# The third pair's last 32 tokens of keys as four loads of 117, 5, 5 and 1 rows, and VectorE's first block at the end of its program

## The chip, the cores and the metric

The kernel runs on one core of a Trainium2 chip. The core has five engines that run their own programs and meet at semaphores: TensorE (PE, matmuls), VectorE (DVE), ScalarE (ACT), GpSimd (POOL) and SyncE (SP), which here only issues transfers. Sixteen DMA engines move data between the chip's main memory (HBM) and the on-chip memory (SBUF), which has 128 partitions, here also called rows. The metric is the device time of one execution in microseconds, and the median of several runs stands for a kernel.

## The reference

One decode step of a transformer block: a vector `c` modulates it, attention reads a cache of 16,384 tokens in 32 heads, and a gated MLP follows. Everything is bf16, for a single token.

```python
mod = (_silu(c) @ w_mod).reshape(c.shape[0], 6, 1, -1)     # c (1, 640), w_mod (640, 3840)
h = _layernorm(x) * (1 + ca) + sa                           # x (1, 1, 640)
q = (h @ wq) as 32 heads of 128                             # wq (640, 4096)
p = softmax(q . k_cache * 128 ** -0.5)                      # k_cache (1, 32, 16384, 128)
x = x + ga * ((p . v_cache) @ wo)                           # v_cache like k_cache, wo (4096, 640)
h = _layernorm(x) * (1 + cb) + sb
x = x + gb * ((silu(h @ w_gate) * (h @ w_up)) @ w_down)     # (640, 1728) twice, (1728, 640)
```

The two caches are 134 MB each; the weights together some 22 MB.

## The kernel before

The heads are worked through in 16 pairs. For one pair the keys are 128 rows of 256 tokens (64 rows a head), each token 128 values of 2 bytes: a row is 64 KB, contiguous in HBM, and a pair is 8.39 MB. `kring` holds the keys of two pairs (slot `p % 2`), `vbuf` the values of one; the last pair's values go into a slot of `kring`.

For each pair VectorE multiplies the keys by the query, spread over all rows in `qbc` (L544 in the two halves c = 0 and 1 of a pair, L562 for the first and the last pair), and folds the products of a token twice (L549, L554; three times in L568). PE sums what is left of each token into scores (`reduce_mm`, L534; `reduce_end`, L576). `largest` and `weigh` make the softmax weights `PZ`, and `pv` (L508) multiplies them with the values. Pairs 1 to 14 run in a loop on PE; on VectorE and ScalarE pairs 0 to 2 are written out and 3 to 14 are a loop of six turns with two pairs in each. After the last pair the output projection, the second layer norm, gate, up and down follow, and two small transfers write the result.

`_Plan` records every operation with what it depends on, and `emit` writes out one program for each engine. Operations of an engine stay in the order of their recording, so nothing is scheduled. A wait goes ahead of the operation that needs it, unless the same engine has waited for as much before. Each transfer counts on a semaphore of its own channel: `("k", p % 2, c)` is that of piece `c` of the keys of pair `p`, so slots share channels. SP issues transfers in recorded order: w_mod, wq, the keys of pair 0 in two pieces (`KCUT`), the keys of pair 1, the values of pair 0, the keys of pair 2, and so on in turns; all of these transfers start at L90. The keys of pair `p` wait for the reduction of pair `p - 2` (`o_R`), the values of pair `p` for `pv` of pair `p - 1`. The last transfers are wo in two pieces, gate, up and five pieces of w_down.

The programs of ScalarE, VectorE and PE stand in blocks of their own: a branch in the main block (L203) leads to `go_act`, `go_dve` and `go_pe`, which come one behind the other in memory. VectorE's program begins with a memset of one row of `rl` (L352, named `one1`); the next is that of `ones_f` (L353). The lines that the prediction's steps touch are `load_k` (L488), `score` (L539, with the wait for the keys at L546), `run` inside `emit` (L139) and the branches (L198 to L206).

Of the kernel before, what the change touches and what calls it, by code (L numbers as in the profile page):

```python
# [37 lines left out]
class _Plan:  # L38
# [7 lines left out]
    def __init__(self, nc, es):  # L46
        self.nc = nc
        self.es = es
        self.ops = []
        self.loop = {}  # L50
        self.turn = None
        self.chans = {e: _Chan(es.enter_context(nc.semaphore("ch_" + e)), 1) for e in self.ENGS if e != "sp"}
        self.dma_chans = {}

# [22 lines left out]
    def op(self, eng, fn, deps=(), name="", chan=None):  # L77
        o = _Op(eng, fn, list(deps), name, len(self.ops), self.loop.get(eng), chan)
        o.sig = chan is not None
        self.ops.append(o)  # L80
        return o
# [23 lines left out]
    def emit(self):  # L105
        for o in self.ops:
            for d in o.deps:
                d.sig = True
                assert d.seq < o.seq, (o.name, d.name)
        per_eng = {e: [o for o in self.ops if o.eng == e] for e in self.ENGS}  # L110
        for e in self.ENGS:
            by_place = {}
            for o in per_eng[e]:
                if o.loop:
                    key, i, n = o.loop
                    by_place.setdefault((key, i), []).append(o)
            for (key, i), ops in by_place.items():
                first = by_place[(key, 0)]
                assert len(first) == len(ops), (key, i)
                for a, b in zip(first, ops):  # L120
                    a.sig = a.sig or b.sig
            for (key, i), ops in by_place.items():
                for a, b in zip(by_place[(key, 0)], ops):
                    b.sig = a.sig
            for o in per_eng[e]:
                if o.sig:
                    ch = o.chan if o.chan is not None else self.chans[e]
                    o.chan = ch
                    ch.count += ch.inc
                    ch.ops.append(o)  # L130
                    o.val = ch.count

        def issue(eng, o):
            ins = o.fn(eng)
            if o.sig:
                assert ins is not None, o.name
                ins.then_inc(o.chan.sem, o.chan.inc)

        def run(name, eng):  # L139
            known = {}  # L140
            ops = per_eng[name]
            at = 0
            while at < len(ops):
                o = ops[at]
                if o.loop is None:
                    for k, (ch, v) in self.needs(o).items():
                        if known.get(k, 0) < v:
                            eng.wait_ge(ch.sem, v)
                            known[k] = v
                    issue(eng, o)  # L150
                    at += 1
                    continue
                key, i, n = o.loop
                end = at
                while end < len(ops) and ops[end].loop and ops[end].loop[0] == key:
                    end += 1
                body = (end - at) // n
                rows = [ops[at + j * body:at + (j + 1) * body] for j in range(n)]
                assert (end - at) == body * n and all(x.loop[1] == j for j, r in enumerate(rows) for x in r)
                done = {}  # L160
                body_needs = []
                for b in range(body):
                    each = [self.needs(r[b]) for r in rows]
                    assert all(set(x) == set(each[1]) for x in each[1:]), rows[0][b].name
                    for k, (ch, v) in each[0].items():
                        if k not in each[1]:

                            assert ch.ops[v // ch.inc - 1].seq < ops[at].seq, rows[0][b].name
                            if known.get(k, 0) < v:
                                eng.wait_ge(ch.sem, v)  # L170
                                known[k] = v
                    waits = []
                    for k, (ch, v1) in each[1].items():
                        step = each[2][k][1] - v1
                        v0 = v1 - step
                        assert all(x[k][1] == v0 + j * step for j, x in enumerate(each) if j), (rows[0][b].name, [x[k][1] for x in each])
                        assert v0 > 0 and step >= 0
                        assert k not in each[0] or each[0][k][1] <= v0, rows[0][b].name
                        assert v0 % ch.inc == 0 and ch.ops[v0 // ch.inc - 1].seq < rows[0][b].seq, rows[0][b].name
                        if known.get(k, 0) >= each[-1][k][1]:  # L180
                            continue
                        if k in done and done[k][1] == step and done[k][0] >= v0:
                            continue
                        done[k] = (v0, step)
                        waits.append((ch, v0, step))
                    body_needs.append(waits)
                with eng.Fori(0, n) as it:
                    self.turn = it
                    for b in range(body):
                        for ch, v0, step in body_needs[b]:  # L190
                            eng.wait_ge(ch.sem, v0 if step == 0 else it * step + v0)  # L191
                        issue(eng, rows[0][b])
                    self.turn = None
                for k, (v0, step) in done.items():
                    known[k] = max(known.get(k, 0), v0 + (n - 1) * step)
                at = end

        nc = self.nc  # L198
        run("sp", nc.sync)
        run("pool", nc.gpsimd)  # L200
        looped = [(nc.scalar, "act"), (nc.vector, "dve"), (nc.tensor, "pe")]
        for eng, name in looped:
            nc.br("go_" + name, engines=[eng.engine])  # L203
        for eng, name in looped:
            with nc.body("go_" + name, valid_engines=[eng.engine]):
                run(name, eng)  # L206


def build(nc, A_x, A_k, A_v, A_wq, A_wo, B_wg, B_wu, B_wd, c_in, w_mod, out):
# [6 lines left out]
    T2 = 2 * S // 128  # L216
# [16 lines left out]
    with es:  # L233
        plan = _Plan(nc, es)
        op, dma = plan.op, plan.dma
# [5 lines left out]
        kring = sb("kring", [128, 2, T2, 128], BF16)  # L241
# [216 lines left out]
        o_qev = []  # L458
# [22 lines left out]
        d_k, d_v = [None] * NP, [None] * NP  # L481
        o_R, o_pv, o_exp, o_nb, o_mx, o_acc, o_ot = ([None] * NP for _ in range(7))
        KCUT = [0, T2 // 2, T2]
        LCUT = [0, T2 // 2, 7 * T2 // 8, T2]
        VCUT = [0, T2]
        v_at = lambda p: vbuf[:] if p < NP - 1 else kring[:, 0]

        def load_k(p):  # L488
            deps = [o_R[p - 2]] if p >= 2 else ([o_mod[1]] if p == 1 else [])
            cuts = KCUT if p == 0 else [0, T2]  # L490
            d_k[p] = [dma(kring[:, p % 2, a:b], k_src(p)[:, a:b], ("k", p % 2, c), deps=deps, name="dma_k%d_%d" % (p, c))
                      for c, (a, b) in enumerate(zip(cuts, cuts[1:]))]

        def load_v(p):
            deps = [o_R[NP - 2]] if p == NP - 1 else [o_pv[p - 1]] if p >= 1 else [o_q[-1]]
# [43 lines left out]
        def score(p, c, between=None):  # L539

            kv4 = kring[:, p % 2].rearrange("p t (a d) -> p t a d", a=2)[:, :, :, QW * c:QW * c + QW]
            def f_mult(e):
                q4 = qbc[:, bass.ds(plan.at(p), 1), :].rearrange("p o (a d) -> p o a d", a=2)[:, :, :, QW * c:QW * c + QW].broadcast_to([128, T2, 2, QW])
                return e.tensor_tensor(out=kv4, in0=kv4, in1=q4, op=ALU.mult)  # L544
            o_m = op(DVE, f_mult,
                     deps=[d_k[p][-1]] + o_qev[p // 2], name="mult%d_%d" % (p, c))  # L546
            if between:
                between[0]()
            o_f = op(DVE, lambda e: e.tensor_tensor(out=kv4[:, :, 0], in0=kv4[:, :, 0], in1=kv4[:, :, 1], op=ALU.add),  # L549
                     deps=[o_m], name="fold%d_%d" % (p, c))  # L550
            if between:
                between[1]()
            lo = kv4[:, :, 0]
            return op(DVE, lambda e: e.tensor_tensor(out=lo[:, :, 0:QR], in0=lo[:, :, 0:QR], in1=lo[:, :, QR:QW], op=ALU.add),  # L554
                      deps=[o_f], name="fold%d_%db" % (p, c))
# [191 lines left out]
        for i, (b, r0, r1) in enumerate(DOWN):  # L747
# [14 lines left out]
            if i == 0:  # L762
# [7 lines left out]
        d_outs = [dma(o_dst[0:2], o_row[31:33, :], "out0", deps=[o_or], name="dma_out0"),  # L770
                  dma(o_dst[2:4], o_row[95:97, :], "out1", deps=[o_or], name="dma_out1", eng="act")]
        op("sp", lambda e: e.nop(), deps=d_outs, name="final_wait")
        plan.emit()
    return plan

# [45 lines left out]
```

## Time and profile before

| | us |
|---|---|
| median of 3 runs | 679.21 (679.02 to 679.4) |
| the profiled execution | 678.87 |
| its span, first to last instruction | 677.6 |
| PE busy with matmuls | 363.6 (54%) |
| VectorE busy | 514.1 (76%) |
| ScalarE busy | 46.4 (7%) |
| HBM read | 290.47 MB, 429 GB/s over the span |

The profile is of one execution. "Busy" is time in which an engine runs instructions of the program. The rows of groups give a line of the kernel, the engine, the operation, output and inputs, then busy time and mean duration, then the engine's idle time ahead of them and what ended it. A row of windows gives, for one stretch of time, the busy time of PE, PE's weight loads, VectorE, ScalarE and GpSimd, the clock granted to PE, the mean busy share of the 16 DMA engines, and their rate. In a short window that share can pass 1, since a packet's time is counted at its start and consecutive packets overlap a little. DMA queues are listed by number: q1 carries what SP issues, q10 what ScalarE issues, q8 and q14 instructions of the programs; packets, megabytes and their share of 16 engines' time follow.

### The profile page before, as it was taken

The page shows a single profiled execution, that of the slowest core. Times are in us where ns is not written, and L with a number is a line of the kernel's source. Part 1 is how long each engine was busy: PE and PEld are TensorE (multiplying, and loading weights), DVE is VectorE, ACT ScalarE, POOL GpSimd, SP SyncE. Part 2 cuts the span into 40 slices and gives each one's busy share as a digit, 9 for nine tenths or more (in the row PEclk, how much of TensorE's full clock was granted, in tenths as well). Part 3 has the DMA queues.
Part 4 walks back from the last instruction along what each step waited for, and adds up shares of the span by engine and source line. Part 5 has one row for each costly group of instructions (what it writes and reads, how often), then busy time and mean ns, then how long its engine had stood idle before and what let it go on. Part 6 is the DMA issues. An engine that isn't in the chain of part 4 may idle for free.

```text
span 677.6 us, 5406 instructions
## 1 busy us (share of the span) xinstructions
PE 363.6 (54%) x2069; PEld 144.5 (21%) x2069; DVE 514.1 (76%) x190; ACT 46.4 (7%) x146; POOL 0.7 (0%) x6
## 2 busy tenths in 40 slices
PE   2420475755728284654818375562828465481776
PEld 1100122221212122221302122121212222130335
DVE  2189997959596896959597795959699695959912
ACT  1120000100000000000000010000000000000010
POOL 0000000000000000000000000000000000000000
PEclk9675565555757565565756556575656556565765
DMA  9999999999999999999999999999999999999997
GB/s 375 440 459 433 433 437 430 433 430 433 433 434 433 433 433 433 433 433 433 433 433 433 433 433 433 433 433 433 433 433 433 433 433 433 433 433 433 430 400 318
DMA packets 6355, 290.58 MB, mean 429 GB/s; under 512 B 714, under 2 KB 972, under 8 KB 1356
## 3 DMA queue, kind: packets, MB, share of 16 engines
q1 hardware_dynamic: 6340, 290.48, 99.3%
q8 instruction: 5, 0.08, 0.0%
q14 instruction: 2, 0.02, 0.0%
q10 hardware_dynamic: 8, 0.00, 0.0%
HBM read 290.47 MB, written 0.00 MB: 429 GB/s over the span
## 4 chain that ended last, share of the span: by engine, by line
DMA 49%; DVE 30%; issue 13%; PE 8%; SPq 0%; DVEq 0%
DMA kring<-in_A_k_cache_dram 45%; DVE kring L544 10%; PE psb L534 7%; DVE kring L549 6%; DVE kring L562 5%; DVE kring L568 5%; DMA kring<-in_B_w_down_dram 4%; DVE kring L554 3%; SPq L90 0%; DVE pm L581 0%; DVE nb L589 0%; PE psb L576 0%; PE psb L758 0%; DVEq L191 0%; DVEq L544 0%
## 5 line engine op out<-in xcount | busy, mean ns | idle before, releaser
L544 DVE TENSOR_TENSOR kring<-kring,qbc 128x16384 bf16<-128x16384 bf16 x28 | 243.3, 8690 | 96.1 <-DMA kring<-in_A_k_cache_dram 96.1
L534 PE MATMUL psb<-kring,ident 128*128 x448 | 197.5, 607 | 120.3 <-DVE kring L554 120.3
L549 DVE TENSOR_TENSOR kring<-kring 128x8192 bf16<-128x8192 bf16 x28 | 123.8, 4421 | 0.5
L534 PEld LDWEIGHTS psb<-kring,ident 128*128 128x128 bf16 x448 | 54.0, 120 | 248.0 <-issue 247.2
L508 PE MATMUL psb<-vbuf,PZ 128*8 128x512 bf16 x960 | 80.9, 511 | 0.0
L585 PE MATMUL psb<-d,bd_f 128*128 128x64 f32 x32 | 11.0, 446 | 118.5 <-ACT d L583 118.5
L554 DVE TENSOR_TENSOR kring<-kring 128x4096 bf16<-128x4096 bf16 x28 | 64.1, 2288 | 0.5
L562 DVE TENSOR_TENSOR kring<-kring,qbc 128x16384 bf16<-128x16384 bf16 (+2 forms) x5 | 34.9, 6981 | 23.4 <-DMA kring<-in_A_k_cache_dram 23.4
L508 PEld LDWEIGHTS psb<-vbuf,PZ 128*8 128x8 bf16 x960 | 26.6, 108 | 58.9 <-issue 49.0
L576 PE MATMUL psb<-kring,ident 128*128 128x256 bf16 (+3 forms) x64 | 14.5, 392 | 43.2 <-DVE kring L568 43.2
L585 PEld LDWEIGHTS psb<-d,bd_f 128*128 128x128 f32 x32 | 8.0, 312 | 120.7 <-DVE pm L581 111.3
L568 DVE TENSOR_TENSOR kring<-kring 128x2048 bf16<-128x2048 bf16 (+7 forms) x15 | 32.2, 2148 | 0.4
L523 PEld LDWEIGHTS psb<-sel,acc_sb 128*128 128x128 f32 x128 | 28.5, 311 | 7.7 <-issue 4.3
L523 PE MATMUL psb<-sel,acc_sb 128*128 128x2 f32 x128 | 25.6, 322 | 1.1 <-ACT acc_sb L514 1.1
L514 ACT ACTIVATE acc_sb<-psb 128x512 f32<-128x512 f32 x16 | 9.6, 598 | 210.7 <-PE psb L508 210.7
L593 ACT ACTIVATE PZ<-psb,nb 64x256 bf16<-64x256 f32 x32 | 15.0, 469 | 64.8 <-DVE nb L589 64.6
L576 PEld LDWEIGHTS psb<-kring,ident 128*128 128x128 bf16 x64 | 6.4, 121 | 50.5 <-DVE kring L568 44.3
L583 ACT ACTIVATE d<-negid,pm 128x64 f32<-128x64 f32 x16 | 5.6, 348 | 153.2 <-DVE pm L581 153.2
L466 PE MATMUL psb<-vbuf,h_col 128*128 128x512 bf16 x40 | 10.9, 443 | 8.6 <-DMA vbuf<-in_A_wq_dram 8.6
L527 ACT ACTIVATE OT_sb<-psb 128x2 f32 (+1 forms) x16 | 2.8, 172 | 152.2 <-PE psb L523 152.2
L581 DVE TENSOR_REDUCE pm<-psb 128x1 f32<-128x256 f32 x16 | 6.7, 419 | 1.2 <-PE psb L576 1.2
L466 PEld LDWEIGHTS psb<-vbuf,h_col 128*128 128x128 bf16 x40 | 4.1, 112 | 15.3 <-DMA vbuf<-in_A_wq_dram 9.0
(105 smaller groups left out, 79.2 us busy)
## 6 DMA issues: line engine op xcount, KB each, us to landing
kring<-in_A_k_cache_dram SPq DMA_DIRECT2D x2, 4096.0 KB, 40.1
vbuf<-in_A_wq_dram SPq DMA_DIRECT2D x1, 5120.0 KB, 25.8
kring<-in_w_mod_dram SPq DMA_DIRECT2D x1, 4800.0 KB, 14.1
vbuf<-in_A_wo_dram SPq DMA_DIRECT2D x1, 3200.0 KB, 20.6
kring<-in_B_w_gate_dram SPq DMA_DIRECT2D x1, 2160.0 KB, 20.6
kring<-in_B_w_up_dram SPq DMA_DIRECT2D x1, 2160.0 KB, 25.4
vbuf<-in_A_wo_dram SPq DMA_DIRECT2D x1, 1920.0 KB, 24.8
kring<-in_B_w_down_dram SPq DMA_DIRECT2D x3, 640.0 KB, 27.6
```

The costliest lines, as they stand in the source:

```text
L466: last = e.matmul(q_ps[b][:, 0:512], lhsT=h_col[:, k:k + 1].broadcast_to([128, 128]), rhs=wq_v[:, k, g * 512:(g + 1) * 512], start=(k == 0 ...
L508: last = e.matmul(acc_ps[32 * s:32 * s + 8, :], lhsT=PZ[:, j, :], rhs=v_at(p)[:, 4 * j:4 * j + 4, :].rearrange("p t d -> p (t d)"), start= ...
L523: last = e.matmul(OT_ps[:, 0:2], lhsT=acc_sb[:, 128 * i:128 * (i + 1)], rhs=sel[:, i:8:4], start=(i == 0), stop=(i == 3))
L534: last = e.matmul(S_ps[:, 0:T2], lhsT=ident[:], rhs=kring[:, bass.ds(plan.slot(p), 1), :, d].rearrange("p o t -> p (o t)"), start=(d == 0) ...
L544: return e.tensor_tensor(out=kv4, in0=kv4, in1=q4, op=ALU.mult)
L549: o_f = op(DVE, lambda e: e.tensor_tensor(out=kv4[:, :, 0], in0=kv4[:, :, 0], in1=kv4[:, :, 1], op=ALU.add), deps=[o_m], name="fold%d_%d" ...
L554: return op(DVE, lambda e: e.tensor_tensor(out=lo[:, :, 0:QR], in0=lo[:, :, 0:QR], in1=lo[:, :, QR:QW], op=ALU.add), deps=[o_f], name="fol ...
L562: o = op(DVE, lambda e: e.tensor_tensor(out=kv, in0=kv, in1=qbc[:, p, :].unsqueeze(1).broadcast_to([128, n, 128]), op=ALU.mult), deps=[d_k ...
L568: o = op(DVE, lambda e, w=w: e.tensor_tensor(out=kv[:, :, 0:w], in0=kv[:, :, 0:w], in1=kv[:, :, w:2 * w], op=ALU.add), deps=[o], name="fol ...
L576: last = e.matmul(S_ps[:, a:b], lhsT=ident[:], rhs=kring[:, p % 2, a:b, d], start=(d == 0), stop=(d == 15))
L585: o_mx[p] = op(PE, lambda e: e.matmul(mx_ps[:, 0:64], lhsT=bd_f[:], rhs=d2[:], start=True, stop=True), deps=[o_d2, o_bd1, o_bd2, o_nb[p - ...
L593: o_exp[p] = op(ACT, lambda e, half=half, ps=ps: e.activation(out=PZ[ps, :, 4 * half:4 * half + 4], in_=S_ps[ps, 0:T2].rearrange("p (c i) ...
```

## The change

Two things change.

The keys of pair 2 (`UP`, the third pair) are loaded in five transfers in place of one. The first brings tokens 0 to 223 of each row, 56 KB a row, for all 128 rows. The last 32 tokens, 8 KB a row, come in four transfers, cut by rows: 0 to 116, 117 to 121, 122 to 126 and 127. By the change's description the DMA engines then take 7, 10 or 11 of these rows. The five transfers are issued one after the other where the one was issued; pieces 2 to 4 have new channels. The first multiply of a pair (c = 0) now waits for all pieces of the pair's keys, the second for the last piece as before. No other load changes.

The other is in `emit`. The program of an engine can be cut into parts ahead of operations named in `cuts`, and the parts can be placed in memory in another sequence (`order`); each part ends with a branch to the one that runs next, and a block with a nop comes last. ScalarE and PE have one part, so they get a branch and a nop at their end. VectorE's program is cut ahead of `ones_f`. Part 1, from `ones_f` on with the loop and all the rest, is placed first; part 0, which is the memset `one1` alone, is placed behind it. VectorE branches from the main block to part 0, back to part 1, and at its end past part 0 to the nop. Its operations run in the same sequence as before.

```diff
-        def run(name, eng):
+        def parts(name, eng):
+
             known = {}
             ops = per_eng[name]
+            out = [[]]
+            todo = out[0]
...
+                if o.name in self.cuts.get(name, ()) and (o.loop is None or o.loop[1] == 0):
+                    todo = []
+                    out.append(todo)
...
-                    issue(eng, o)
+                    todo.append(lambda o=o: issue(eng, o))
...
+        programs = [(nc.scalar, "act"), (nc.vector, "dve"), (nc.tensor, "pe")]
+        work = {name: parts(name, eng) for eng, name in programs}
+        for eng, name in programs:
+            nc.br(name + "_0", engines=[eng.engine])
+        for eng, name in programs:
+            n = len(work[name])
+            for i in self.order.get(name, range(n)):
+                with nc.body("%s_%d" % (name, i), valid_engines=[eng.engine]):
+                    for f in work[name][i]:
+                        f()
+                    go = eng.br("%s_%d" % (name, i + 1))
+            with nc.body("%s_%d" % (name, n), valid_engines=[eng.engine]):
+                eng.nop()
...
+        UP, UT, UROWS = 2, T2 - 32, [0, 117, 122, 127, 128]
...
-            d_k[p] = [dma(kring[:, p % 2, a:b], k_src(p)[:, a:b], ("k", p % 2, c), deps=deps, name="dma_k%d_%d" % (p, c))
-                      for c, (a, b) in enumerate(zip(cuts, cuts[1:]))]
+            rows = [(0, 128, a, b) for a, b in zip(cuts, cuts[1:])]
+            if p == UP:
+                rows = [(0, 128, 0, UT)] + [(r, s, UT, T2) for r, s in zip(UROWS, UROWS[1:])]
+            d_k[p] = [dma(kring[r:s, p % 2, a:b], k_src(p)[r:s, a:b], ("k", p % 2, c), deps=deps, name="dma_k%d_%d" % (p, c))
+                      for c, (r, s, a, b) in enumerate(rows)]
...
-                     deps=[d_k[p][-1]] + o_qev[p // 2], name="mult%d_%d" % (p, c))
+                     deps=(d_k[p] if c == 0 else [d_k[p][-1]]) + o_qev[p // 2], name="mult%d_%d" % (p, c))
...
+        plan.cuts = {"dve": ("ones_f",)}
+        plan.order = {"dve": (1, 0)}
         plan.emit()
```

More of the change, by code (lines that the diff above doesn't have):

```diff
@@ L51, in __init__ @@
         self.turn = None
+        self.cuts = {}
+        self.order = {}
         self.chans = {e: _Chan(es.enter_context(nc.semaphore("ch_" + e)), 1) for e in self.ENGS if e != "sp"}
@@ L137, in issue, with wait, loop @@
                 ins.then_inc(o.chan.sem, o.chan.inc)
-        def run(name, eng):
+        def parts(name, eng):
             known = {}
             ops = per_eng[name]
+            out = [[]]
+            todo = out[0]
+            def wait(ch, v):
+                todo.append(lambda: eng.wait_ge(ch.sem, v))
+            def loop(n, body_needs, row):
+                with eng.Fori(0, n) as it:
+                    self.turn = it
+                    for waits, o in zip(body_needs, row):
+                        for ch, v0, step in waits:
+                            eng.wait_ge(ch.sem, v0 if step == 0 else it * step + v0)
+                        issue(eng, o)
+                    self.turn = None
             at = 0
@@ L147, in run @@
                         if known.get(k, 0) < v:
-                            eng.wait_ge(ch.sem, v)
+                            wait(ch, v)
                             known[k] = v
-                    issue(eng, o)
+                    todo.append(lambda o=o: issue(eng, o))
                     at += 1
@@ L169, in run @@
                             if known.get(k, 0) < v:
-                                eng.wait_ge(ch.sem, v)
+                                wait(ch, v)
                                 known[k] = v
@@ L186, in run @@
                     body_needs.append(waits)
[L187 to L193, printed above, removed]
+                todo.append(lambda n=n, w=body_needs, r=rows[0]: loop(n, w, r))
                 for k, (v0, step) in done.items():
@@ L196, in run @@
                 at = end
+            return out
         nc = self.nc
[L199 to L206, printed above, removed]
+        for eng, name in ((nc.sync, "sp"), (nc.gpsimd, "pool")):
+            for todo in parts(name, eng):
+                for f in todo:
+                    f()
[8 more added lines that the diff above has]
+                    for f in work[name][i]:
+                        f()
+                    go = eng.br("%s_%d" % (name, i + 1))
+            with nc.body("%s_%d" % (name, n), valid_engines=[eng.engine]):
+                eng.nop()
 def build(nc, A_x, A_k, A_v, A_wq, A_wo, B_wg, B_wu, B_wd, c_in, w_mod, out):
```

## The prediction

> **What bounds the kernel now.** I read the page's busy times first, then the windows of the long middle, then the chain that ended last, and at last the windows of the final two microseconds.
>
> ```profile
> span 677.6 us, 5406 instructions
> PE 363.6 (54%) x2069; PEld 144.5 (21%) x2069; DVE 514.1 (76%) x190; ACT 46.4 (7%) x146; POOL 0.7 (0%) x6
> HBM read 290.47 MB, written 0.00 MB: 429 GB/s over the span
> ```
>
> No compute engine is full. The next row (a window; its last two columns are the share of time in which the 16 DMA engines were busy and their rate) says what is: from 187 to 606 us all 16 are busy all the time.
>
> ```profile
> 187.00:606.00 419.00, 233.89 (x1153) 85.95 (x1154) 337.28 (x88) 24.47 (x76) 0.00 (x0) 0.57 1.00 433
> ...
> L544 DVE TENSOR_TENSOR kring<-kring,qbc 128x16384 bf16<-128x16384 bf16 x28 | 243.3, 8690 | 96.1 <-DMA kring<-in_A_k_cache_dram 96.1
> ```
>
> 290.47 MB at 433 GB/s are 670.8 us, so 6.8 us of the span are start and end. VectorE, the busiest compute engine, waits 96.1 us for keys in L544 alone. So only two things can move the time: the work of the DMA engine that is done last, and what follows its last transfer. The chain at the end:
>
> ```profile
> 645.86 28.65 DMA kring<-in_B_w_down_dram
> 674.51 0.04 issue
> 674.55 1.08 PE psb L758 x14
> ```
>
> The w_down transfer ends the wait at 674.51, and all after it follows directly. How the DMA engines run dry there is in the windows of 0.2 us:
>
> ```profile
> 673.20:673.40 0.20, 0.20 (x11) 0.12 (x6) 0.00 (x0) 0.00 (x0) 0.00 (x0) 0.50 1.02 328
> 673.40:673.60 0.20, 0.20 (x9) 0.20 (x12) 0.11 (x1) 0.00 (x0) 0.00 (x0) 0.50 0.48 176
> 673.60:673.80 0.20, 0.20 (x16) 0.18 (x8) 0.05 (x1) 0.00 (x0) 0.00 (x0) 0.50 0.42 160
> 673.80:674.00 0.20, 0.20 (x12) 0.00 (x0) 0.00 (x0) 0.00 (x0) 0.00 (x0) 0.50 0.26 99
> 674.00:674.20 0.20, 0.11 (x4) 0.00 (x0) 0.00 (x0) 0.00 (x0) 0.00 (x0) 0.50 0.30 106
> 674.20:674.40 0.20, 0.00 (x0) 0.00 (x0) 0.00 (x0) 0.00 (x0) 0.00 (x0) 0.50 0.27 96
> 674.40:674.60 0.20, 0.05 (x4) 0.05 (x8) 0.00 (x0) 0.00 (x0) 0.00 (x0) 0.50 0.25 77
> 674.60:674.80 0.20, 0.20 (x10) 0.20 (x14) 0.00 (x0) 0.00 (x0) 0.00 (x0) 0.50 0.07 19
> ```
>
> A share of 0.25 to 0.30 is four to five of 16 engines: nearly a microsecond after most are done, about four still work, and the kernel waits for these. From 673.4 on the shares add up to 2.05 x 0.2 us x 16 = 6.6 us of engine time. Spread over all 16 that is 0.41 us: the end could come at 673.8 instead of 674.7. **0.9 us is the ceiling** of what any rebalancing can gain, and no row needs more than one late engine to lose. About 0.2% (1.36 us) is what a measurement of this kernel can tell from no change; the ceiling lies under it.
>
> Why four are late: the kernel's instructions come over the same engines.
>
> ```profile
> q8 instruction: 4, 0.07, 0.0%
> q14 instruction: 2, 0.02, 0.0%
> ```
>
> These are the DMA queues up to 673 us: four packets of 16 KB, two of 8 KB, while four engines are late. The counts fit; that each late one carried a 16 KB packet is inferred. In the windows around one of each kind (108.2 to 109 us, then 149.4 to 150) their prices show:
>
> ```profile
> q8 instruction: 1, 0.02, 7.6%
> ...
> q14 instruction: 1, 0.01, 3.4%
> ```
>
> 7.6% of 16 engines over 0.8 us is 0.97 us of one engine; 3.4% over 0.6 us is 0.33 us.
>
> **The change part by part.** (1) *Rows moved between DMA engines.* 128 rows of 8 KB (32 tokens x 256 B) are eight per engine if spread evenly. As described, eleven engines take seven, four take ten and one takes eleven. One engine moves 433/16 = 27.1 GB/s, so a row costs 8192/27.1 = 0.303 us: eleven engines are relieved by 0.30 us, four loaded by 0.61, one by 0.91. Each engine works through its backlog without a pause, so this offset stays until the end. If all late engines are among the eleven, the end comes 0.30 us sooner. The five then end up to 0.91 us later than before; by the share of 0.48 half the engines are done by about 673.5, 1.1 us ahead of the last, so the five fit in if they belong to these.
>
> (2) *More packets.* Each engine gets seven to eleven packets more. The price of one is seen where rows are short (5 KB):
>
> ```profile
> 670.00:671.30 1.30, 1.30 (x44) 1.30 (x43) 0.00 (x0) 0.00 (x0) 0.00 (x0) 0.50 1.02 414
> ```
>
> 5120 B x 16 at 414 GB/s are 198 ns, at 433 they would be 189: 9 ns a packet, 0.06 us for seven. Bounds: 0 (the share is 1.02, so the rate may be off by as much) and 0.1 us.
>
> (3) *Four more issues on SP.* K of pair 2 and what is queued behind it:
>
> ```profile
> 77.28 0.33 SPq L90 DMA_DIRECT2D kring<-in_A_k_cache_dram  x1
> 98.36 0.33 SPq L90 DMA_DIRECT2D vbuf<-in_A_v_cache_dram  x1
> ...
> kring<-in_A_k_cache_dram SPq DMA_DIRECT2D x15, 38.7
> ```
>
> 4 x 0.33 = 1.3 us before SP waits again for the V load at 98.36, 21 us off: nothing. Without that cover each issue would delay V by 0.33 us, and even that would meet a backlog: a load needs 8.39 MB / 433 GB/s = 19.4 us and lands after 38.7, so 19.3 us of other work are queued ahead of it.
>
> (4) *The first multiply of pair 2 waits for all five loads.*
>
> ```profile
> 105.53 8.69 DVE L544 TENSOR_TENSOR kring<-kring,qbc 128x16384 bf16<-128x16384 bf16 x1 [4.39 <-DMA kring<-in_A_k_cache_dram]
> 144.90 8.69 DVE L544 TENSOR_TENSOR kring<-kring,qbc 128x16384 bf16<-128x16384 bf16 x1 [8.29 <-DMA kring<-in_A_k_cache_dram]
> ```
>
> It may start up to 0.9 us later. Behind it stand pair 2's folds, the reduction on PE, and K of pair 4, which that releases; this goes into the 19.3 us of backlog. VectorE has 8.29 us to catch up before pair 3. Cost nothing.
>
> (5) *VectorE's first instruction at the end of its program.* VectorE jumps forward by its whole program and back. If the far end has not been fetched, it waits.
>
> ```profile
> 0.93 0.17 DVE L353 MEMSET ones_f<- 128x128 f32 x1
> 8.42 0.17 DVE L374 TENSOR_SCALAR dd<-ec 128x5 f32<-128x5 f32 x1 [5.80 <-ACT ec L372]
> 14.95 3.56 PE L427 MATMUL psb<-kring,silu_c 128*32 128x480 bf16 x40 [4.61 <-DMA kring<-in_w_mod_dram]
> ```
>
> 5.80 us of idling hide it, and then the wait for w_mod, 4.61 us on PE. No row shows such a stall. Below I bound it by 0; above by two jumps, each behind one packet of w_mod in flight (38,400 B at 27.1 GB/s, 1.42 us) and a fetch at the 16 KB packet's 0.97 us: 4.8 us, still under 5.80. Both ends are hidden; I take the nearer row, one fetch, and nothing for it. Were the cover gone, w_mod's product would be late, and after it K of pair 1, which has the backlog still. Queued behind VectorE's first block are only its own memsets. [...]
>
> A packet like those of q14 for the far end of the program would cost the engine that carries it 0.33 us by its own row, up to 0.97 by that of the larger packet. I take 0 for the end, as 12 of 16 engines are not late. (6) A branch and a nop end three programs; the output's landing, 1.0 us, covers them:
>
> ```profile
> SPq L772 <- DMA out_dram<-o_row: 1.0, 1, 1.0
> ```
>
> **Sum.** -0.30 + 0.06 = -0.24 us. PE stood idle for 0.44 us at the last wait, so it can follow this.
>
> ```profile
> 674.55 0.86 PE L758 MATMUL psb<-kring,gu_col 128*32 128x160 bf16 x20 [0.44 <-DMA kring<-in_B_w_down_dram]
> ```
>
> The profiled run took 678.87 us (span 677.6 and 1.27 around it), 0.34 under the median of 679.21. 678.87 - 0.24 = 678.63; on the median's level 678.97. I say **679.0 us**, by itself 678.6 to 679.4 with the runs' own spread.
>
> **The rivals.** *A: 117 rows are not cut into 7 and 8.* The change doesn't do what it says, if a load uses only as many engines as divide its rows: 117 = 13 x 9. Then thirteen engines take nine rows and three none; with the small loads one engine has twelve, four eleven, eight nine. Only three engines are relieved, and four are late, so at least one late engine gets more: +0.30 if it is among the eight, +0.91 or +1.21 if among the five, each +0.07. Time 679.6, 680.2 or 680.5; middle 679.9. For it: 117 is no multiple of 16, and every large load in the trace has 128 rows, so no row shows an uneven cut. Against it: only the description's own figures. [...]
>
> *B: the cut is as described, but a late engine is among the five.* It gets +0.61 or +0.91, +0.08 for packets: 679.9 or 680.2, slower from one such engine on. For it: four late, five loaded, and no view names an engine. Drawn blindly, none of four would be among five of 16 with a chance of (11x10x9x8)/(16x15x14x13) = 18%. Against it: a fifth 16 KB packet runs at the very end (window 673.3 to 673.6), too late to matter,
>
> ```profile
> q8 instruction: 1, 0.02, 22.8%
> ```
>
> and as far as packet times can be strung together it runs on the engine that carried the one-row load of x. If a one-row load takes the first engine, and these packets take engines in turn, the four before it fell on the last ones, which are relieved. That is an inference, not a view: of the 61% that the forecast and B share, B keeps 18.
>
> *C: a fetch for VectorE's far block falls on a late engine.* -0.24 + 0.33 to 0.97: 679.3 to 679.9. For it: the q14 rows; against: one in four.
>
> *D: a larger gain,* if the new places in VectorE's program also take a packet off a late engine (0.33 to 0.97): 678.4 with 0.6 us more, near the ceiling.
>
> **How the numbers follow.** Forecast 43%, A 25%, B 18%, C 9%, D 3%, and 2% for something outside (a stall that isn't covered). The range leaves out less than 2 in 10: 678.4 (D) to 680.3 (B, and A but for its worst case). Faster by over 0.2% means under 677.85, below the ceiling: 2%. Slower by over 0.2%, over 680.57, needs A's worst case and C together, or an uncovered stall: 6%. Within 0.2%: 92%.
>
> **What would show it.** Right: the staircase of shares at the end is shorter, with its four-engine step ending about 0.25 us sooner; the w_down wait ends the chain as before. A shows as a step at which one or a few engines are busy alone, and in a K load of pair 2 that lands up to 1 us late; B as a step of one or two engines, later than 674.7. C or D: another place of the q14 packets, with fewer of them after the start. VectorE's memsets some microseconds late, with L374's idle time shortened by as much, confirm part 5. I am wrong in kind if the middle no longer shows a share of 1.00 at 433 GB/s, or if the chain at the end runs over anything but w_down.

## The result, and the profile after

| | before | after |
|---|---|---|
| median, us (6 runs each, side by side) | 679.23 (679.02 to 679.69) | 683.47 (682.39 to 684.53) |
| ratio, 95% interval | | 1.0062 (1.005 to 1.0075) |
| the profiled execution, us | 678.87 | 682.39 |
| its span, us | 677.6 | 681.1 |

The change costs 4.2 us. The profiled execution is the quickest of its six, so the profile has 3.5 us of them to show. First the page of the kernel after: its span, the rate in 40 slices of 17 us, the packets, and VectorE's wait for keys.

```profile
span 681.1 us, 5414 instructions
...
GB/s 383 428 457 435 424 398 399 431 431 431 435 432 435 435 435 431 431 431 435 435 431 431 443 435 439 435 431 435 431 435 431 435 431 431 431 431 435 434 408 301
...
DMA packets 6507, 290.58 MB, mean 427 GB/s; under 512 B 738, under 2 KB 996, under 8 KB 1380
...
HBM read 290.47 MB, written 0.00 MB: 426 GB/s over the span
...
L573 DVE TENSOR_TENSOR kring<-kring,qbc 128x16384 bf16<-128x16384 bf16 x28 | 243.3, 8688 | 99.4 <-DMA kring<-in_A_k_cache_dram 99.4
```

The same two rows of the page of the kernel before:

```profile
GB/s 375 440 459 433 433 437 430 433 430 433 433 434 433 433 433 433 433 433 433 433 433 433 433 433 433 433 433 433 433 433 433 433 433 433 433 433 433 430 400 318
...
DMA packets 6355, 290.58 MB, mean 429 GB/s; under 512 B 714, under 2 KB 972, under 8 KB 1356
```

The rows of rates are where to look first. Slices five to seven (68 to 119 us) fell from 433, 437 and 430 to 424, 398 and 399 GB/s: 79 GB/s short over 17 us are 3.1 us at 433. After that both rows stay near 433. VectorE's wait for keys grew by 3.3 us, from 96.1 to 99.4. So bytes flowed too slowly in one place, and nothing later made up for it.

The packets tell how the 117 rows were cut. There are 152 more; 128 are the tail's rows, and 24 are very short (738 against 714 under 512 B; by the packet records all 24 have 4 B). 24 is 13 + 5 + 5 + 1, and the landing events of the traces split it that way: every load of 128 rows raises its semaphore sixteen times as it lands, the load of 117 rows did so 13 times (105.48 to 108.02 us), those of 5, 5 and 1 rows 5, 5 and 1 times. The sixteen of a full load would have made it 16 + 5 + 5 + 1 = 27. I read this as one for each engine that takes part, so that the 117 rows ran on thirteen engines, with nine rows each if these share them evenly; that is an inference, since no view names an engine.

What goes on in the slow stretch is in the windows of both kernels; the columns are those of the windows shown before, the last two the busy share of the DMA engines and their rate. After:

```profile
97.00:112.00 15.00, 10.95 (x58) 4.52 (x48) 6.74 (x3) 0.77 (x2) 0.00 (x0) 0.61 0.97 340
...
105.00:107.00 2.00, 2.00 (x6) 0.59 (x5) 0.00 (x0) 0.00 (x0) 0.00 (x0) 0.50 0.90 246
107.00:109.00 2.00, 2.00 (x8) 1.14 (x6) 0.00 (x0) 0.00 (x0) 0.00 (x0) 0.50 1.05 410
...
187.00:606.00 419.00, 229.43 (x1149) 85.16 (x1150) 340.81 (x88) 24.64 (x77) 0.00 (x0) 0.58 1.00 433
```

Before:

```profile
97.00:112.00 15.00, 9.87 (x52) 4.16 (x40) 10.58 (x3) 0.77 (x2) 0.00 (x0) 0.70 0.97 416
...
105.00:107.00 2.00, 2.00 (x6) 0.62 (x5) 1.47 (x1) 0.00 (x0) 0.00 (x0) 0.50 1.21 524
```

A window of 2 us is uneven, since a packet counts where it starts, but over 15 us the reading is firm: the engines are as busy as before (0.97 both times), and they move 340 GB/s, not 416. That is 2.6 us at 433. **They are not idle; their packets take longer.** The middle, from 187 us on, is untouched.

The packet records of the traces (start, duration and size of each packet) show which ones, between 90 and 130 us. An 8 KB packet of the tail took 0.47 us in the mean. Where the tail is one load of 128 rows (E3 below) it takes 0.31, which is about the price of a row in the prediction. And 20 of the 161 packets of 64 KB, all of other loads, took over a tenth longer than their usual 2.42 us, the longest 4.78; before it was 1 of 258. Spread over 16 engines, either comes to 1.3 us. So about half of the time lost there was lost by packets that the change doesn't touch.

The timeline of VectorE after, at the multiplies of pairs 2 and 3 (start, duration, operation, idle time ahead of it and what ended that):

```profile
109.63 8.69 DVE L573 TENSOR_TENSOR kring<-kring,qbc 128x16384 bf16<-128x16384 bf16 x1 [8.23 <-DMA kring<-in_A_k_cache_dram]
...
147.99 8.69 DVE L573 TENSOR_TENSOR kring<-kring,qbc 128x16384 bf16<-128x16384 bf16 x1 [7.29 <-DMA kring<-in_A_k_cache_dram]
```

Pair 2 begins 4.1 us later than before (105.53). Pair 3, whose load is the same in both kernels, begins 3.1 us later (144.90). The shift goes through to the end; the chain that ended last, after:

```profile
649.44 28.62 DMA kring<-in_B_w_down_dram
678.06 0.04 issue
678.11 1.07 PE psb L787 x21
```

w_down ends the wait at 678.06, before at 674.51: 3.55 us later, the whole difference of the spans. How the engines run dry there, after:

```profile
676.20:676.60 0.40, 0.39 (x16) 0.39 (x16) 0.00 (x0) 0.00 (x0) 0.00 (x0) 0.50 0.48 186
676.60:677.00 0.40, 0.40 (x17) 0.13 (x13) 0.00 (x0) 0.00 (x0) 0.00 (x0) 0.50 0.37 144
677.00:677.40 0.40, 0.40 (x17) 0.37 (x16) 0.16 (x1) 0.00 (x0) 0.00 (x0) 0.50 0.36 128
677.40:677.80 0.40, 0.30 (x12) 0.00 (x0) 0.00 (x0) 0.00 (x0) 0.00 (x0) 0.50 0.16 56
677.80:678.20 0.40, 0.10 (x4) 0.10 (x8) 0.00 (x0) 0.00 (x0) 0.00 (x0) 0.50 0.09 30
```

The last step is now one or two engines (a share of 0.09 is 1.4 of 16), where it was four. From a share near a half to the end of the wait it takes 1.5 to 1.9 us (from 676.2 or 676.6), before 1.1 (from 673.4): the engines end further apart, by 0.4 to 0.8 us. The rest of the 3.55, about 3 us, is near the 2.6 us by which packets were longer.

The other edit shows at the start of VectorE's program:

```profile
1.43 0.09 DVE L377 MEMSET rl<- 1x32 f32 x1 [1.43 <-PEq L837]
1.77 0.17 DVE L378 MEMSET ones_f<- 128x128 f32 x1 [0.26 <-issue]
...
8.51 0.17 DVE L399 TENSOR_SCALAR dd<-ec 128x5 f32<-128x5 f32 x1 [5.05 <-ACT ec L397]
```

`ones_f` begins 0.84 us later than before, and the idle time ahead of L399 is shorter by 0.75 us, still 5.05. An instruction packet that ran at 149.4 us before now runs near the start; these are the queues from 3 to 5 us, with nothing of q14 there before:

```profile
q1 hardware_dynamic: 16, 0.61, 72.4%
q14 instruction: 1, 0.01, 1.2%
```

### The profile page after: what moved, and what is told of

Same layout as the page of the kernel before. It is cut to its first block, busy times and chain, and to the rows that moved or that the text cites. A ratio compares the mean times of both kernels' runs of the same rounds, so it can differ in the third digit from the quotient of the medians.

```text
span 681.1 us, 5414 instructions
## 1 busy us (share of the span) xinstructions
PE 361.1 (53%) x2068; PEld 143.9 (21%) x2069; DVE 514.1 (75%) x190; ACT 46.4 (7%) x146; POOL 0.7 (0%) x6
## 4 chain that ended last, share of the span: by engine, by line
DMA 49%; DVE 30%; issue 12%; PE 8%; SPq 0%; DVEq 0%
DMA kring<-in_A_k_cache_dram 45%; DVE kring L573 10%; PE psb L563 7%; DVE kring L578 6%; DVE kring L591 5%; DVE kring L597 5%; DMA kring<-in_B_w_down_dram 4%; DVE kring L583 3%; SPq L92 0%; DVE pm L610 0%; DVE nb L618 0%; PE psb L605 0%; PE psb L787 0%; DVEq L156 0%; DVEq L573 0%
## 5 line engine op out<-in xcount | busy, mean ns | idle before, releaser
L573 DVE TENSOR_TENSOR kring<-kring,qbc 128x16384 bf16<-128x16384 bf16 x28 | 243.3, 8688 | 99.4 <-DMA kring<-in_A_k_cache_dram 99.4
L537 PE MATMUL psb<-vbuf,PZ 128*8 128x512 bf16 x960 | 79.4, 504 | 0.0
```

The lines of the kernel that those rows point to most:

```text
L537: last = e.matmul(acc_ps[32 * s:32 * s + 8, :], lhsT=PZ[:, j, :], rhs=v_at(p)[:, 4 * j:4 * j + 4, :].rearrange("p t d -> p (t d)"), start= ...
```

## The experiments

All are made from the changed kernel, and each was timed beside the kernel before, whose median lay between 679.16 and 679.32 us in the four series. Loads are said to collide below when the share of the DMA engines stays near 1 or above while their rate falls, as above.

### Which of the two edits

E1 keeps VectorE's new order and loads pair 2 in one transfer. E2 is the reverse.

```diff
E1
-        UP, UT, UROWS = 2, T2 - 32, [0, 117, 122, 127, 128]
+        UP, UT, UROWS = None, T2 - 32, [0, 117, 122, 127, 128]
E2
-        plan.cuts = {"dve": ("ones_f",)}
-        plan.order = {"dve": (1, 0)}
```

> The placing of VectorE's first block alone, every load as before. Theory of the rows (the cost comes from the four tail loads of pair 2, by counts or by contention): 679.0 to 679.6, with the early 8 KB instruction packet worth at most 0.4 us. Rival (the branch to a far block costs the time): 682 to 684.

> The four tail loads alone, VectorE's program in its old sequence (with the new branches at the ends of the programs). Theory of the rows: 682 to 684, as with both edits. Rival (the far block): 679.0 to 679.6.

E1 took 679.34 us, ratio 1.0001 (0.9991 to 1.001); E2 682.57, ratio 1.0052 (1.0035 to 1.0069). The loads alone bring the loss, and VectorE's far block alone costs nothing that can be measured. E2 lost 3.3 us and the change 4.2, but their runs overlap (682.30 to 683.47 and 682.39 to 684.53), so whether the block adds anything beside the loads is not settled.

### Short rows, uneven counts, or few rows in a transfer

E3 loads the tail of 8 KB rows for all 128 rows in one transfer. E4 cuts it at row 112, so that sixteen engines take seven rows and then one: uneven cuts, but eight rows for every engine. The theory of contention in the expectations takes it that an engine has usual rows, which it gets in every load of 128 rows; that is the author's estimate, since no view names an engine.

```diff
E3
+        UP, UT, UROWS = 2, T2 - 32, [0, 128]
E4
+        UP, UT, UROWS = 2, T2 - 32, [0, 112, 128]
```

> Both edits, but the last 32 tokens of pair 2 in one load of all 128 rows, eight to an engine: 8 KB packets as in the change, even counts, each engine its usual rows. Theory of small packets (8 KB pieces are slow in themselves): 682 to 684. Theory of uneven counts and theory of contention (engines that write rows which are not their usual ones get in each other's way): 679.2 to 679.6, 0.07 us for eight packets more.

> Both edits, but the tail as loads of 112 and 16 rows: seven and one to each engine, eight in sum, so the counts are even, while most rows go through another engine than in a load of 128 rows. Theory of uneven counts: 679.2 to 679.7. Theory of contention: 681 to 683, since most of the loss in the trace of the change (busy DMA engines at 246 to 295 GB/s from 101 to 107 us) should stay.

E3 took 679.18 us, ratio 0.9999 (0.999 to 1.0009): 144 more packets and one more transfer cost nothing. E4 took 682.14, ratio 1.0041 (1.0027 to 1.0055), although every engine has as many bytes as in E3 if each load is shared evenly (its two loads bring 16 short packets each). So balance is not the main thing. The window from 101 to 107 us, in the kernels before and after:

```profile
101.00:107.00 6.00, 5.72 (x14) 1.77 (x15) 1.61 (x2) 0.00 (x0) 0.00 (x0) 0.67 1.11 481
...
101.00:107.00 6.00, 5.46 (x13) 1.69 (x14) 0.40 (x1) 0.00 (x0) 0.00 (x0) 0.55 1.12 307
```

(E4's expectation has 246 to 295 GB/s for it; that leaves out 103 to 105 us, at 381.) In E3:

```profile
101.00:107.00 6.00, 5.26 (x13) 1.63 (x14) 1.83 (x2) 0.00 (x0) 0.00 (x0) 0.68 1.20 512
```

in E4:

```profile
101.00:107.00 6.00, 5.36 (x13) 1.67 (x14) 0.50 (x1) 0.00 (x0) 0.00 (x0) 0.62 1.24 333
```

The same share, and two thirds of the rate. E7 then gives the engines the counts that the change aimed at: 112 rows on sixteen engines and 5 + 5 + 5 + 1, which makes eleven engines with 7, four with 10 and one with 11, if the small loads fall on the same engines. Its 32 additional short packets fit 16 + 5 + 5 + 5 + 1; which engines they are, no view says. E8 doubles the bytes of the change's tail.

```diff
E7
+        UP, UT, UROWS = 2, T2 - 32, [0, 112, 117, 122, 127, 128]
E8
+        UP, UT, UROWS = 2, T2 - 64, [0, 117, 122, 127, 128]
```

> Both edits, the tail as 112, 5, 5, 5 and 1 rows, so that the engines do take 7, 10 or 11 rows. Theory of counts, as predicted: 679.0. Theory of contention: 681.5 to 684, the 112 rows alone keep most of the loss.

> Both edits, the tail twice as long: the last 64 tokens in loads of 117, 5, 5 and 1 rows of 16 KB. Theory of contention: the loss grows with the bytes that go through the wrong engine, about double of the change's 4.2 us: 686 to 689. If the loss is a fixed cost of the uneven loads or of their number: 683 to 684.

E7 took 682.6 us, ratio 1.005 (1.0033 to 1.0067): the cut that the change aimed at lost 3.4 us too. E8 took 688.16, ratio 1.0131 (1.0115 to 1.0146): 8.8 us for twice the bytes, against 4.2. The loss goes with the bytes.

### Neighbouring rows

By now the theory was that the loss comes from which rows are on the move together. E5 and E6 cut the tail into two and four blocks of neighbouring rows, with eight rows an engine each time if the loads are shared evenly. E9 makes four loads of 32 rows too, but each takes every fourth row; from there on the rows of a load are written as slices, and the line that issues the loads is fitted to that.

```diff
E5
+        UP, UT, UROWS = 2, T2 - 32, [0, 64, 128]
E6
+        UP, UT, UROWS = 2, T2 - 32, [0, 32, 64, 96, 128]
E9
+                rows = [(slice(0, 128), 0, UT)] + [(slice(r, 128, 4), UT, T2) for r in range(4)]
...
```

> Both edits, the tail as two loads of 64 rows, four rows to each engine each time. If engines only lose where 7 or 9 rows don't fit some pattern: 679.2 to 679.6. Theory of contention (a stretch of rows takes in data at a fixed rate, whoever brings it): all 16 engines push 0.52 MB into half of the rows, twice, so 2.4 us of transfer take up to 4.8: 680.5 to 681.8.

> Both edits, the tail as four loads of 32 neighbouring rows, two rows to each engine each time, counts even. Theory of contention: all 16 engines push into a quarter of the rows. If an engine's usual rows are eight neighbours, four times the 2.4 us of transfer at most: up to 686.5. If they are spread over two places 32 rows apart, 32 neighbours still belong to eight engines and the loss is as with 64 rows: 680.5 to 681.8. Theory of uneven counts: 679.2 to 679.8.

> Both edits, the tail as four loads of 32 rows again, but each takes every fourth row (0, 4, 8 to 124, then 1, 5 and so on): as many transfers, packets and engines as with 32 neighbours, spread over all rows. Theory of contention for neighbouring rows: 679.2 to 680.2. If the number of transfers or two rows an engine cost the time: as with 32 neighbours.

| | us | ratio (95%) |
|---|---|---|
| E5, two blocks of 64 | 683.13 | 1.0058 (1.0041 to 1.0074) |
| E6, four blocks of 32 | 683.32 | 1.006 (1.0043 to 1.0077) |
| E9, every fourth row, four loads | 679.37 | 1.0003 (0.9994 to 1.0013) |

E5 and E6 took longer than the 680.5 to 681.8 us that their expectations gave for a tail at half its rate, and E6 stayed far from its other end, 686.5. E6 and E9 have the same number of transfers, rows, packets and waits, and as many rows in each load. Only the rows differ. In the window from 101 to 107 us E6 shows

```profile
101.00:107.00 6.00, 5.16 (x13) 1.51 (x14) 0.70 (x1) 0.00 (x0) 0.00 (x0) 0.80 1.34 315
```

and E9

```profile
101.00:107.00 6.00, 5.17 (x13) 1.53 (x14) 1.65 (x2) 0.00 (x0) 0.00 (x0) 0.77 1.16 496
```

### Reading side or writing side

A row of the load is one place in HBM and one partition of SBUF. E10 reads every fourth row and writes 32 neighbouring partitions; E11 reads 32 neighbouring rows and writes every fourth partition.

```diff
E10
+                rows = [...] + [(slice(32 * r, 32 * r + 32), slice(r, 128, 4), UT, T2) for r in range(4)]
E11
+                rows = [...] + [(slice(r, 128, 4), slice(32 * r, 32 * r + 32), UT, T2) for r in range(4)]
+            d_k[p] = [dma(kring[w, p % 2, a:b], k_src(p)[r, a:b], ("k", p % 2, c), deps=deps, name="dma_k%d_%d" % (p, c))
+                      for c, (w, r, a, b) in enumerate(rows)]
```

> Four loads of 32 rows that read every fourth row from HBM but write 32 neighbouring rows of SBUF. The last 32 tokens of pair 2 thereby land in other rows, so some of its keys are scored under another head and token. If engines collide where they write (SBUF): 683.0 to 683.6, as with 32 neighbours on both sides. If they collide where they read (HBM): 679.2 to 679.8.

> The reverse: four loads that read 32 neighbouring rows from HBM and write every fourth row of SBUF, again with the last 32 tokens of pair 2 in other rows. Collision at the writing side: 679.2 to 679.8. At the reading side: 683.0 to 683.6.

E10 took 683.09 us, ratio 1.0056 (1.0041 to 1.0071); E11 679.26, ratio 1.0 (0.999 to 1.0009). With E6 and E9 these make a square of reading and writing: both kernels that write neighbouring partitions lose, both that write every fourth one don't, whatever they read. The collision is on the writing side. The window from 101 to 107 us in E10:

```profile
101.00:107.00 6.00, 5.39 (x13) 1.65 (x14) 0.47 (x1) 0.00 (x0) 0.00 (x0) 0.66 1.32 332
```

and in E11:

```profile
101.00:107.00 6.00, 5.36 (x13) 1.63 (x14) 1.51 (x2) 0.00 (x0) 0.00 (x0) 0.81 1.21 513
```

### Which partitions collide

E12 tries for the change's counts (7, 10 and 11) without collisions: loads of 16 rows, eight apart, in the belief, an estimate of the author's, that an engine's eight neighbours in a full load are the unit that collides. E13 makes eight blocks of 16 neighbours.

```diff
E12
+                rows = [(slice(0, 128), 0, UT)] + [(slice(r, 128, 8), UT, T2) for r in range(7)] + [(slice(7 + 8 * i, min(128, 7 + 8 * j), 8), UT, T2) for i, j in ((0, 5), (5, 10), (10, 15), (15, 16))]
...
E13
+                rows = [(slice(0, 128), 0, UT)] + [(slice(r, r + 16), UT, T2) for r in range(0, 128, 16)]
...
```

> Both edits, the tail as seven loads of 16 rows, each eight rows apart (rows 0, 8, 16 and so on, then 1, 9 and so on, up to 6), and the 16 rows that are left (7, 15 and so on) as 5, 5, 5 and 1: the counts of 7, 10 and 11 with only 16 of 128 rows through an engine that isn't their usual one. As predicted by counts: 0.24 us under the kernel before, 679.0. Theory of contention: about 16/128 of the 3 us that 112 neighbouring rows lost, and no gain from the counts since a stretch of rows takes in no more per microsecond: 679.2 to 679.8.

> Both edits, the tail as eight loads of 16 neighbouring rows, one row to each engine each time. If what is limited is a group of a few neighbouring rows that takes in one engine's rate: 16 rows are half as many groups as 32, so four engines share one; 8 KB packets of some 1.2 us in the middle (32 and 64 neighbours gave 0.6), 7.3 us of extra transfer at the least, 686.5 to 692. If any collision costs a factor of two, however many engines take part: 683 to 684.

Both went otherwise. E12 took 683.33 us, ratio 1.0055 (1.0041 to 1.0068), a full loss: rows eight apart collide as well (a share of 1.34 at 300 GB/s from 101 to 107 us). E13 took 684.23, ratio 1.0069 (1.0054 to 1.0085), 5.0 us more than before: worse than blocks of 32 or 64, but between what a factor of two and one of four would give: its 8 KB packets took 0.77 us in the mean, 2.5 times the 0.31 of E3. Its window from 101 to 107 us has the lowest rate of all:

```profile
101.00:107.00 6.00, 5.45 (x13) 1.63 (x14) 0.41 (x1) 0.00 (x0) 0.00 (x0) 0.77 0.97 158
```

A unit of eight neighbours doesn't fit these: by it E12 would be clean. What the runs give is a list and no rule. Tails written in blocks of 16, 32 or 64 neighbours, or in rows eight apart, lost 3.8 to 5.0 us (E13, E6, E10, E5, E12); 32 rows four apart lost nothing (E9, E11). The tail is 1.05 MB, 2.4 us at 433 GB/s. E5 and E6 lost 4.0 and 4.2, and the packet records divide this: the tail's 8 KB packets took 0.60 us in the mean in place of 0.31, which is 2.3 us over 16 engines in both; packets of 56 and 64 KB took longer too, up to 4.3 us, which is another 1.3 and 1.6 us. E9, E11 and E3 show neither.

Blocks of up to 64 neighbours don't settle why the change itself lost. 112 and 117 neighbouring rows are nearly all of the 128, and yet E4, E7, E2 and the change lose 2.9 to 4.2 us. (Of E4's 2.9 its other 16 rows, an eighth of E13's tail, would make some 0.6, an estimate from E13's 5.0.) Why they lose was not shown: no view says which engine writes which row, and no row of any trace says why a packet takes longer.

E14 is a second try at the counts 7, 10 and 11: three loads of every fourth row, and only the last 32 rows in loads that collide.

```diff
E14
+                rows = [(slice(0, 128), 0, UT)] + [(slice(r, 128, 4), UT, T2) for r in range(3)] + [(slice(3, 64, 4), UT, T2)] + [(slice(67 + 4 * i, min(128, 67 + 4 * j), 4), UT, T2) for i, j in ((0, 5), (5, 10), (10, 15), (15, 16))]
...
```

> Both edits, counts of 7, 10 and 11 again, with fewer collisions: three loads of 32 rows four apart (which lost nothing), then rows 3, 7 to 63 as one load of 16, and rows 67, 71 to 127 as 5, 5, 5 and 1. Theory of counts, as predicted: 679.0, and up to 679.5 with the collisions of the last 32 rows. Theory of contention: the last 32 rows (a quarter of the tail) lose a quarter of the 4 us, and the counts gain nothing: 679.8 to 680.5.

E14 took 680.4 us, ratio 1.0017 (1.0008 to 1.0026): 1.1 us lost with a quarter of the tail in colliding loads, where E12 lost 4.0, with all of its tail in such loads. The window from 101 to 107 us lies between E6 and E9:

```profile
101.00:107.00 6.00, 5.24 (x13) 1.64 (x14) 0.62 (x1) 0.00 (x0) 0.00 (x0) 0.63 1.10 369
```

No gain from the rebalancing shows in it, and none of the kernels is faster than the one before; E1, E3, E9 and E11 can't be told from it.

**What stays open.** What it is in a set of partitions that makes engines slow: E13 fits neither factor of its expectation, how a colliding load holds up the packets of other loads wasn't tried by itself, and which engine writes which rows of 112 or 117 isn't seen. And the part that uneven counts have in the 4.2 us: the kernels with thirteen engines (the change 4.2, E2 3.3) and those with sixteen (E4 2.9, E7 3.4) differ by about as much as their runs scatter, so 1.3 us is the most that the medians leave for it.

## Why the prediction was wrong

The forecast was 679.0 us, the range 678.4 to 680.3, and 92% for no difference that can be told. It came to 683.47.

**The step that failed is the price of a row in part (1)**, "a row costs 8192/27.1 = 0.303 us", with the sentence behind it, that each engine works through its backlog without a pause. In the change a row of the tail took 0.47 us in the mean, which is 1.3 us over 16 engines, and the packets of other loads, whose price the sum left unchanged, lost as much again. The step takes for granted that a busy DMA engine moves 27.1 GB/s whatever it writes to. The trace of before supports that only for loads of 128 rows, and the prediction itself noted, in rival A, that every large load has 128 rows. It used this to bound how many rows an engine takes, and not what a row costs. By the same rule as the other unseen prices (bounds from both sides), the row's price needed an upper end, and all the cases (forecast, A, B, C) used the lower one. The runs in its place: with the tail in loads of 117, 112, 64 or 32 neighbouring rows, in blocks of 16, or in rows eight apart, the kernel took 2.9 to 5.0 us more; with all 128 rows in one load, or 32 four apart where they are written (E3, E9, E11), it took no more, and a row took 0.31 us.

**The cut (rival A, 25%)** was right on the 117 rows: they landed with 13 events, read above as thirteen engines. No run shows on which engines the small loads fell, so A's counts of twelve and eleven rows stay an estimate. A's price was wrong for the reason above: it gave 0.4 to 1.3 us. And its cut was not the cause: with the counts as described, E7 lost 3.4 us all the same. The single late engines that A was to show at the end are there, but the longer end accounts for 0.4 to 0.8 of 3.55 us, and it need not come from the counts: in E4, with eight rows for each engine, the share is down at 0.42 some 1.8 us ahead of the wait's end.

**The bound** was read rightly, as far as it went: all engines busy, so that any time lost by them comes out at the end in full, and nothing absorbs it. But a share of 1.00 was read as a rate. The sign that the prediction set for being wrong in kind, a middle no longer at 1.00 and 433 GB/s, did not appear, though it was wrong in kind: from 187 us on the middle is as before, and the loss lay ahead of that, where the changed load runs. **The gain of 0.24 us and the ceiling of 0.9** were never tested by themselves: no cut that moves counts as described was free of collisions, and E14, nearest to that, lost 1.1. By the prediction's own rows the ceiling is 0.7 us: the wait ends at 674.51, and 0.9 counts to 674.7. **B and D** are left open as well. One reading under B isn't shown: that the fifth 16 KB packet came too late to matter. By its record it ran from 673.30 to 674.40 us, 0.1 us ahead of the wait's end, so its engine may be one of the late ones.

**(2) More packets, 0.06 us:** right within the measurement, E3 with 144 more differs by -0.07 us. **(3) Four more issues, nothing:** right, SP's five issues took 1.79 us in place of 0.33, and E9 has as many and differs by 0.21 us, within its interval. **(4) The first multiply of pair 2:** it came 4.1 us later, not 0.9. As the prediction has it, VectorE could take this: it still waits 7.29 us for pair 3's keys, which are late themselves. **(5) VectorE's block at the far end, nothing:** right. The memsets came up to 0.84 us late, not some microseconds, the 5.80 us of idle time shrank to 5.05, and E1 can't be told from before. That a fetch held VectorE up was not shown: `one1` itself began 0.57 us later (1.43 in place of 0.86), 0.26 us of idling followed it, and the packet of q14 ran only at 3.92 us, after `ones_f` at 1.77. **C**, a fetch on a late engine: one packet of q14 did move from 149.4 us to the start (3.9 us in the change, 4.3 in E1), at no cost that shows in E1. **(6) The branches and nops:** E1 contains them; nothing.

## What to carry to other kernels

Where the DMA engines bound a kernel, read their rate next to their busy share: a busy engine can be a slow one (here a share of 0.97 came with 416 GB/s before and with 340 after), and an engine's bytes at its own best rate are only the lower end of a load's price, which can also fall on the packets of other loads. Before a load is cut by rows, ask which partitions the pieces write; if it must be cut, pieces that take every fourth row cost nothing here (E9, E11), while blocks of neighbours cost 4 us for 1 MB. A price that the trace shows for one shape of load only has an unknown upper end for another shape, even where the engine is the same.

## What the runs showed of the hardware

Two kernels whose tails read the same rows and differ in the partitions that they write are 4.2 us (E6 and E11) and 3.6 us (E10 and E9) apart, each taken against the kernel before in its own series, for 1.05 MB, which takes 2.4 us at 433 GB/s. A load of 16, 32, 64 or 112 rows does not simply use a part of the machine: by the short packets all sixteen engines take part, their packets and those of other loads take longer where the rows collide (0.52 to 0.77 us in the mean in place of 0.31 for 8 KB, up to 4.9 in place of 2.42 for 64 KB, by the packet records of E4, E5, E6, E7 and E13), and the engines count as busy all the while. Two of the kernels that collide also scatter more from run to run, 682.39 to 684.53 us for the change and 686.21 to 688.38 for E8, against 679.02 to 679.69 for the kernel before; E5, at 682.82 to 683.27, doesn't.
